# Attention features and a feed-forward block on one core: projections in 64-row tiles, query features turned on VectorE, key features on GpSimd, and one list of tasks

## The chip, the cores and the metric

The kernel runs on one core of one Trainium2 chip. The metric is the device time of one launch in microseconds (us). Three runs of the kernel before gave 123.22, 123.42 and 123.79 us; the median is 123.42 us.

## The reference, cut to what matters

```python
# q, k, v: (B=4, H=4, S=1088, D=32); S1, S2: (8, 32); all fp32
def phi(x):                                   # 64 features of a token and head
    a = einsum('rd,bhsd->bhsr', S1, x)        # 8 numbers
    b = einsum('rd,bhsd->bhsr', S2, x)        # 8 numbers
    return outer(a, b).reshape(..., 64)
q_p, k_p = phi(q), phi(k)
kv  = einsum('bhsf,bhsd->bhfd', k_p, v)       # 64 x 32 for a batch and head
z   = sum(k_p, axis=2)                        # 64
num = einsum('bhsf,bhfd->bhsd', q_p, kv)
den = einsum('bhsf,bhf->bhs', q_p, z)[..., None] + 1e-06
x   = (num / den).transpose(0, 2, 1, 3).reshape(4352, 128)
h   = x @ w_in                                # 128 x 2048
out = (h * sigmoid(h)) @ w_out                # 2048 x 128, fp32 out
```

## The kernel before

There are four batches of 1088 tokens. The keys and queries of a batch are loaded as `Kx[b]` and `Qx[b]`, 128 partitions (4 heads x 32 rows) by 34 x 32 numbers. VectorE transposes them in blocks of 32 x 32 (`transpose_cols`, L154) to `KT` and `QT`, in which the partitions hold 4 heads x 32 features. TensorE projects them with weights of 128 x 32 (`project_k` L203, `project_q` L210) in four column groups, and VectorE turns the result back to tokens on partitions (`tokens`, L218). VectorE forms the key features `kp` by a product with broadcast operands (`outer`, L194, 2304 numbers on each partition for a batch), TensorE sums `kv` over tokens (`sum_kv`, L234). The denominators come from a third set of query weights `WQb`, made from the sum of the keys (`sum_z`, `query_weights`, `mask_weights`). The query features `qp` are formed on VectorE, turned by TensorE with an identity (`turn`, L263, 72 instructions in all), copied out of PSUM by VectorE (`qpt`), multiplied with `KVbd` on TensorE (`numerators`, L274) and copied by VectorE to `xT` (128 x 4352, bf16), the input of the feed-forward block.

The feed-forward block goes over `xT` in chunks of 256, 512, 320, six times 512, and 192 tokens. A chunk has steps (`Chunk.hidden`, L317): a pair of matmuls into one of two PSUM buffers `h_ps`, a SiLU on ScalarE of 1024 numbers on each partition (fewer in the short chunks) into one of eight buffers `g`; `Chunk.output` (L329) sums the output in `o_ps`; at a chunk's end VectorE turns it (L341) and `store` issues four DMAs or more on SyncE's queue (L301).

The order is written out by hand. The code before step 0 of `feed_forward` makes the first 256 tokens; the rest of batch 0 and batches 1 to 3 are generators that are advanced once a step, beginning at steps 0, 5, 19 and 35. Every engine's instructions stand in the trace in the order in which the code issues them (`tc.manual_schedule()`).

The loads: `begin` (L82) starts a DMA that may wait for another one's landing. SyncE's queue has the keys and queries, the values of batch 0 and `w_in`; from batch 1 on each load waits for one before it. GpSimd's queue has memsets, then `w_out` (cast to bf16 by the DMA), then the values of batches 1, 2 and 3 (`load_v`, L140), where batch 1 waits for the last half of `w_in`, batch 2 for the queries of batch 1, and batch 3 for the queries of batch 2. Nothing stands behind them on GpSimd:

```python
    prev = wi1
    for b in range(1, B):
        load_v(nc.gpsimd, b, Vb[b], prev)
        kb = load_kq(nc.sync, b, k, Kx, after=prev)
        prev = load_kq(nc.sync, b, q, Qx, after=q0b if b == 1 else kb)
```

Of the kernel before, what the change touches and what calls it, by code (L numbers as in the profile page):

```python
# [9 lines left out]
FP32 = mybir.dt.float32  # L10
# [6 lines left out]
def bcast(ap: AP, axis: int, count: int) -> AP:  # L17
    pairs = [list(p) for p in ap.ap]
    pairs.insert(axis, [0, count])
    return AP(tensor=ap.tensor, offset=ap.offset, ap=pairs)  # L20
# [3 lines left out]
def kernel(  # L24
# [11 lines left out]
    nc = tc.nc  # L36
    P = nc.NUM_PARTITIONS

    B, H, S, D = q.shape
    R = S1.shape[0]  # L40
    HR = H * R
# [5 lines left out]
    NY = S // 32  # L47
    NC = 9
    YA = 24
    assert DM == P and HR == 32 and S == 32 * NY and 3 * NC < NY <= 4 * NC  # L50

    const = ctx.enter_context(tc.tile_pool(name="const", bufs=1))
    work = ctx.enter_context(tc.tile_pool(name="work", bufs=2))
    moeg = ctx.enter_context(tc.tile_pool(name="moeg", bufs=8))
    outb = ctx.enter_context(tc.tile_pool(name="outb", bufs=2))
    psH = ctx.enter_context(tc.tile_pool(name="psH", bufs=2, space=bass.MemoryType.PSUM))
    psO = ctx.enter_context(tc.tile_pool(name="psO", bufs=1, space=bass.MemoryType.PSUM))
    psP = ctx.enter_context(tc.tile_pool(name="psP", bufs=2, space=bass.MemoryType.PSUM))
    psA = ctx.enter_context(tc.tile_pool(name="psA", bufs=1, space=bass.MemoryType.PSUM))

    ctx.enter_context(tc.manual_schedule())

    Kx = [const.tile([P, NY, D], FP32, name=f"Kx{b}") for b in range(B)]
    Qx = [const.tile([P, NY, D], FP32, name=f"Qx{b}") for b in range(B)]
    Vx = const.tile([P, H, NC, D], FP32, name="Vx")
    Vb = [const.tile([P, H, NC, D], BF16, name=f"Vb{b}") for b in range(B)]
    KT = [const.tile([P, 4 * NC * 32], FP32, name=f"KT{i}") for i in range(2)]
    QT = [const.tile([P, 4 * NC * 32], FP32, name=f"QT{i}") for i in range(2)]
    PQ = [const.tile([P, 3, NC, HR], FP32, name=f"PQ{i}") for i in range(2)]
    AW = [const.tile([P, NC * H, R + 1], FP32, name=f"AW{i}") for i in range(2)]  # L70
    WQb = [const.tile([P, HR], FP32, name=f"WQb{b}") for b in range(B)]
    KVbd = [const.tile([P, 2, 2 * D], BF16, name=f"KVbd{b}") for b in range(B)]
    w_in_f = const.tile([P, DFF], FP32, name="w_in_f")
    w_in_bf = const.tile([P, DFF], BF16, name="w_in_bf")
    w_out_bf = const.tile([P, NJ, P], BF16, name="w_out_bf")
    xT = const.tile([P, NTOK], BF16, name="xT")

    S12 = const.tile([R, 2, D], FP32, name="S12")  # L80

    def begin(eng, dst, src, after=None):  # L82
        ins = eng.dma_start(dst, src)  # L83
        if after is not None:
            tc.add_manual_dep(ins.ins, after.ins.name, mybir.DependencyInfo(
                mybir.DependencyClass.Sync, mybir.DependencyReason.DATA), reason="order of loads")
        return ins

    def load_kq(eng, b, src, dst, y0=0, y1=NY, after=None):
        return begin(eng, dst[b][:, y0:y1, :].rearrange("p a d -> p (a d)"),  # L90
                     AP(tensor=src.tensor, offset=src[b, 0, y0].offset,
                        ap=[[NY * D, P], [1, (y1 - y0) * D]]), after)

    def load_v(eng, b, dst, after=None):
        for c in range(4):
            n = min(NC, NY - c * NC)
            ins = begin(eng, dst[32 * c: 32 * (c + 1), :, :n, :].rearrange("p h n d -> p h (n d)"),
                        AP(tensor=v.tensor, offset=v[b, 0, c * NC].offset,
                           ap=[[NY * D, 32], [S * D, H], [1, n * D]]), after)
        return ins  # L100

    nc.scalar.dma_start(S12[:, 0, :], S1)
    nc.sync.dma_start(S12[:, 1, :], S2)
    k0a = load_kq(nc.sync, 0, k, Kx, 0, 2 * NC)
    k0b = load_kq(nc.scalar, 0, k, Kx, 2 * NC, NY)
    q0a = load_kq(nc.sync, 0, q, Qx, 0, YA)
    v0 = load_v(nc.sync, 0, Vx, k0a)
    half = DFF // 2
    wi0 = begin(nc.sync, w_in_f[:, :half], moe_w_in[:, :half], q0a)
    wi1 = begin(nc.sync, w_in_f[:, half:], moe_w_in[:, half:])  # L110
    q0b = load_kq(nc.sync, 0, q, Qx, YA, NY, v0)


    warm = const.tile([P, 1], FP32, name="warm")
    nc.gpsimd.memset(warm, 0.0)
    ident32 = const.tile([32, 32], FP32, name="ident32")
    make_identity(nc, ident32)
    hmask = const.tile([P, H, R], FP32, name="hmask")
    nc.gpsimd.memset(hmask, 0.0)
    for h in range(H):  # L120
        nc.gpsimd.memset(hmask[D * h: D * (h + 1), h, :], 1.0)
    nc.gpsimd.memset(KT[0][:, NY * 32:], 0.0)
    nc.gpsimd.memset(QT[0][:, NY * 32:], 0.0)
    nc.gpsimd.memset(Vx[96:P, :, NY - 3 * NC: NC, :], 0.0)
    nc.gpsimd.memset(KVbd[0], 0.0)
    for i in range(2):
        nc.gpsimd.memset(AW[i][:, :, R:], 1e-6)
    ident_bf = const.tile([P, P], BF16, name="ident_bf")
    make_identity(nc, ident_bf)
    nc.gpsimd.memset(KT[1][:, NY * 32:], 0.0)  # L130
    nc.gpsimd.memset(QT[1][:, NY * 32:], 0.0)
    for b in range(1, B):
        nc.gpsimd.memset(KVbd[b], 0.0)
        nc.gpsimd.memset(Vb[b][96:P, :, NY - 3 * NC: NC, :], 0.0)
    wo = begin(nc.gpsimd, w_out_bf, moe_w_out.rearrange("(j p) m -> p j m", p=P), v0)


    prev = wi1
    for b in range(1, B):
        load_v(nc.gpsimd, b, Vb[b], prev)  # L140
        kb = load_kq(nc.sync, b, k, Kx, after=prev)
        prev = load_kq(nc.sync, b, q, Qx, after=q0b if b == 1 else kb)

    nc.scalar.activation(out=warm, in_=warm, func=ACT.Silu)
    REP32 = const.tile([32, 4, 32], FP32, name="REP32")
    nc.vector.tensor_copy(out=REP32, in_=bcast(ident32[:, :], 1, 4))
    rep32 = REP32.rearrange("p h d -> p (h d)")
    REPJ = const.tile([R, 4, R], FP32, name="REPJ")
    nc.vector.tensor_copy(out=REPJ, in_=bcast(ident32[:R, :R], 1, 4))
    hm = const.tile([HR, H], FP32, name="hm")  # L150
    nc.vector.tensor_reduce(out=hm, in_=ident32.rearrange("p (h j) -> p h j", h=H),
                            axis=AX.X, op=ALU.add)

    def transpose_cols(dst, src, b, c0, c1):  # L154
        nc.vector.transpose(out=dst[:, c0:c1],  # L155
                            in_=src[b].rearrange("p a d -> p (a d)")[:, c0:c1])


    st_ps = psA.tile([P, 2 * R], FP32, name="st_ps", tag="acc")
    nc.tensor.transpose(st_ps[:D, 0:R], S12[:, 0, :], ident32[:R, :R])  # L160
    nc.tensor.transpose(st_ps[:D, R:2 * R], S12[:, 1, :], ident32[:R, :R])
    ST_sb = const.tile([D, 2 * R], FP32, name="ST_sb")
    nc.vector.tensor_copy(out=ST_sb, in_=st_ps[:D, :])
    rep_ps = psP.tile([P, 2 * R], FP32, name="rep_ps", tag="proj")
    nc.tensor.matmul(rep_ps, rep32, ST_sb, start=True, stop=True)
    s2_ps = psA.tile([HR, D], FP32, name="s2_ps", tag="acc")
    nc.tensor.matmul(s2_ps, REPJ.rearrange("p h j -> p (h j)"), S12[:, 1, :],
                     start=True, stop=True)
    transpose_cols(KT[0], Kx, 0, 0, 2 * NC * 32)
    WK = const.tile([P, 2, H, R], FP32, name="WK")  # L170
    for i in range(2):
        nc.vector.tensor_tensor(out=WK[:, i], in0=bcast(rep_ps[:, i * R: (i + 1) * R], 1, H),  # L172
                                in1=hmask, op=ALU.mult)
    wk = [WK[:, i].rearrange("p h i -> p (h i)") for i in range(2)]
    transpose_cols(KT[0], Kx, 0, 2 * NC * 32, S)


    L1 = const.tile([HR, H, D], FP32, name="L1")
    nc.vector.tensor_tensor(out=L1, in0=bcast(s2_ps[:, :], 1, H), in1=bcast(hm[:, :], 2, D),
                            op=ALU.mult)  # L180
    l4_ps = psA.tile([P, P], FP32, name="l4_ps", tag="acc")
    L4 = const.tile([P, P], FP32, name="L4")

    def l4():
        nc.tensor.matmul(l4_ps, rep32, L1.rearrange("p h d -> p (h d)"), start=True, stop=True)  # L185
        nc.scalar.activation(out=L4, in_=l4_ps, func=ACT.Copy)  # L186

    def vcopy(out_, in_):
        nc.vector.tensor_copy(out=out_, in_=in_)  # L189

    def acopy(out_, in_):
        nc.scalar.activation(out=out_, in_=in_, func=ACT.Copy)

    def outer(dst, a, bb):  # L194
        nc.vector.tensor_tensor(  # L195
            out=dst.rearrange("p n h i j -> p (n h) i j"),
            in0=bcast(a.rearrange("p n (h i) -> p (n h) i", h=H), 3, R),
            in1=bcast(bb.rearrange("p n (h j) -> p (n h) j", h=H), 2, R), op=ALU.mult)

# [343 lines left out]
```

## Time and profile before

| what | value |
|---|---|
| median of 3 runs | 123.42 us (123.22 to 123.79) |
| profiled execution, first to last instruction (span) | 122.1 us; no time of its own is given beside it, and the median of the runs is 1.3 us longer |
| PE, DVE, ACT, POOL busy | 97.7, 68.7, 74.2, 11.8 us |
| SiLU on ACT (L325): busy, idle before them | 67.7 us in 72, 31.1 us |
| first SiLU starts, last one ends | 19.18 us, 116.91 us |
| mean granted TensorE clock | 0.983 |

PE is TensorE, DVE is VectorE, ACT is ScalarE, POOL is GpSimd, SP is SyncE. Matmuls are pipelined: a pair of 512 columns shows 0.59 us from the first start to the last end while pairs follow each other every 0.43 us, so busy time of PE is not work at its peak.

### The profile page before, as it was taken

What the parts mean: (1) busy time and instruction counts of PE and PEld (TensorE: products, weight loads), DVE (VectorE), ACT (ScalarE), POOL (GpSimd) and SP (SyncE); (2) the same over time, 40 slices, a digit from 0 to 9 for tenths busy, and PEclk for the clock granted to TensorE, in tenths of its full rate; (3) what the DMA queues carried; (4) which work ended last, traced back from release to release, by engine and by line L of the source; (5) the groups of instructions that cost most, each with busy time, mean ns of one, the idle gap of its engine ahead of it and who ended that gap; (6) DMA issues with size and microseconds to landing.
All of it is one profiled execution on the core that took longest, in us unless ns stands there. A gap on an engine that the chain in (4) does not pass through costs nothing.

```text
span 122.1 us, 2269 instructions
## 1 busy us (share of the span) xinstructions
PE 97.7 (80%) x884; PEld 50.5 (41%) x896; DVE 68.7 (56%) x126; ACT 74.2 (61%) x83; POOL 11.8 (10%) x41
## 2 busy tenths in 40 slices
PE   0397849969999649899982999999838989989940
PEld 0265627644445435435432244445304434434630
DVE  1367693499945996993369649953398430020210
ACT  4005466666576725466981379667843899999920
POOL 6604510701600000000000000000000000000000
PEclk9999999999999999999999599999999999999998
DMA  2799997691994500030013000500031005013151
GB/s 52 263 222 319 182 358 127 195 205 62 222 173 109 87 2 0 2 57 0 3 21 65 0 0 5 86 0 5 0 59 27 0 0 86 0 21 53 17 94 27
DMA packets 24314, 9.80 MB, mean 80 GB/s; under 512 B 21104, under 2 KB 22896, under 8 KB 24304
## 3 DMA queue, kind: packets, MB, share of 16 engines
q1 hardware_dynamic: 20352, 8.03, 26.0%
q0 software_dynamic: 3792, 1.36, 9.8%
q10 hardware_dynamic: 160, 0.26, 0.6%
q8 instruction: 7, 0.11, 0.4%
q14 instruction: 3, 0.02, 0.1%
HBM read 8.78 MB, written 2.23 MB: 90 GB/s over the span
## 4 chain that ended last, share of the span: by engine, by line
PE 59%; DVE 22%; ACT 7%; DMA 5%; issue 4%; SPq 0%; DVEq 0%; ACTq 0%
PE h_ps L322 20%; PE o_ps L335 17%; DVE qp L195 7%; ACT g L325 5%; PE qpt_ps L268 4%; PE pq_ps L214 3%; PE num_ps L277 3%; PE pk_ps L206 3%; DMA Kx<-in_k_dram 3%; DVE o_tt L341 3%; PE h_ps L206 2%; DVE PQ L219 2%; DVE qpt L189 2%; DVE den L256 2%; DVE AW L254 2%
## 5 line engine op out<-in xcount | busy, mean ns | idle before, releaser
L325 ACT ACTIVATE g<-h_ps 128x1024 bf16<-128x1024 f32 (+2 forms) x72 | 67.7, 980 | 31.1 <-PE h_ps L322 25.5
L322 PE MATMUL h_ps<-xT,w_in_bf 128*128 128x512 bf16 (+3 forms) x151 | 41.5, 365 | 1.9 <-ACT g L325 1.4
L335 PE MATMUL o_ps<-g,w_out_bf 128*128 128x512 bf16 (+3 forms) x157 | 39.3, 349 | 0.5
L335 PEld LDWEIGHTS <-w_out_bf 128*128 128x128 bf16 x160 | 15.5, 98 | 14.8 <-issue 1.1
L322 PEld LDWEIGHTS <-w_in_bf 128*128 128x128 bf16 x160 | 13.1, 103 | 15.9 <-issue 11.1
L341 DVE STREAM_TRANSPOSE o_tt<-o_ps 128x512 f32<-128x512 f32 (+3 forms) x10 | 6.3, 631 | 20.6 <-PE o_ps L335 18.8
L268 PE MATMUL qpt_ps<-ident_bf,qp 128*128 128x128 bf16 (+1 forms) x72 | 6.7, 235 | 9.2 <-DVE qp L195 8.5
L195 DVE TENSOR_TENSOR kp<-pk 128x1280 bf16<-128x1280 f32 (+1 forms) x8 | 10.8, 1352 | 0.2
L195 DVE TENSOR_TENSOR qp<-aqs,PQ 128x1024 bf16<-128x1024 f32 (+3 forms) x9 | 10.8, 1223 | 0.2
L268 PEld LDWEIGHTS <-qp 128*128 128x128 bf16 (+1 forms) x72 | 5.0, 106 | 12.8 <-DVE qp L195 10.0
L189 DVE COPY qpt<-qpt_ps 128x1024 bf16<-128x1024 bf16 (+2 forms) x11 | 5.9, 540 | 5.7 <-PE qpt_ps L268 5.7
L189 DVE CAST xT<-num_ps 128x512 bf16<-128x512 f32 (+2 forms) x11 | 5.8, 531 | 4.8 <-PE num_ps L277 4.8
L83 POOL DMA_DIRECT2D Vb<-in_v_dram x12 | 6.5, 548 | 15.1 <-DMA Qx<-in_q_dram 12.3
L155 DVE STREAM_TRANSPOSE KT<-Kx 128x1088 f32<-128x1088 f32 (+2 forms) x5 | 5.4, 1075 | 2.1 <-DMA Kx<-in_k_dram 2.1
L277 PE MATMUL num_ps<-qpt,KVbd 128*64 128x512 bf16 (+3 forms) x24 | 4.7, 383 | 2.2 <-DVE qpt L189 1.4
L155 DVE STREAM_TRANSPOSE QT<-Qx 128x512 f32<-128x512 f32 (+3 forms) x8 | 5.7, 718 | 0.0
L277 PEld LDWEIGHTS <-KVbd 128*64 128x64 bf16 x24 | 1.9, 111 | 7.0 <-issue 6.9
L214 PE MATMUL pq_ps<-QT,WK 128*32 128x128 f32 (+2 forms) x112 | 4.7, 284 | 0.0
L206 PE MATMUL h_ps<-KT,WK 128*32 128x160 f32 (+1 forms) x32 | 2.8, 448 | 2.1 <-DVE WK L172 2.1
L206 PE MATMUL pk_ps<-KT,WK 128*32 128x160 f32 (+1 forms) x96 | 4.2, 292 | 0.1
L186 ACT ACTIVATE L<-l_ps 128x128 f32<-128x128 f32 x1 | 0.3, 277 | 6.3 <-PE l_ps L185 6.3
L219 DVE STREAM_TRANSPOSE PQ<-pq_ps 128x256 f32<-128x256 f32 (+2 forms) x7 | 3.3, 470 | 1.0 <-PE pq_ps L214 1.0
(73 smaller groups left out, 61.6 us busy)
## 6 DMA issues: line engine op xcount, KB each, us to landing
Kx<-in_k_dram SPq DMA_DIRECT2D x3, 544.0 KB, 4.8
Qx<-in_q_dram SPq DMA_DIRECT2D x3, 544.0 KB, 6.1
out_dram<-o_tt SPq DMA_DIRECT2D x20, 64.0 KB, 1.9
w_in_f<-in_moe_w_in_dram SPq DMA_DIRECT2D x2, 512.0 KB, 6.1
Vb<-in_v_dram POOLq DMA_DIRECT2D x9, 72.0 KB, 3.8
w_out_bf<-in_moe_w_out_dram POOLq DMA_DIRECT2D x1, 512.0 KB, 8.2
Vx<-in_v_dram SPq DMA_DIRECT2D x3, 144.0 KB, 2.8
Qx<-in_q_dram SPq DMA_DIRECT2D x1, 384.0 KB, 4.9
```

Source lines behind the costliest of these rows:

```text
L83: ins = eng.dma_start(dst, src)
L155: nc.vector.transpose(out=dst[:, c0:c1], in_=src[b].rearrange("p a d -> p (a d)")[:, c0:c1])
L189: nc.vector.tensor_copy(out=out_, in_=in_)
L195: nc.vector.tensor_tensor(out=dst.rearrange("p n h i j -> p (n h) i j"), in0=bcast(a.rearrange("p n (h i) -> p (n h) i", h=H), 3, R), in1= ...
L206: nc.tensor.matmul(ps[32 * c: 32 * (c + 1), i, :], w, kt[:, (c * NC + n0) * 32: (c * NC + n1) * 32], start=True, stop=True, tile_position= ...
L214: nc.tensor.matmul(ps[32 * c: 32 * (c + 1), i, :].rearrange("p (n x) -> p n x", x=32), w, q4[:, n0:n1, c, :], start=True, stop=True, tile_ ...
L268: nc.tensor.transpose(qpt_ps[:, p, (n - n0) * P: (n - n0) * P + np_], qp[:np_, n, 2 * p: 2 * p + 2].rearrange("p h i j -> p (h i j)"), ide ...
L277: nc.tensor.matmul(num_ps[64 * p: 64 * (p + 1), :ncol], KVbd[b][:, p, :], qpt[:, p, :ncol], start=True, stop=True, tile_position=(0, 64 * p))
L322: nc.tensor.matmul(h[:, i, :self.ntok], w_in_bf[:, j * P: (j + 1) * P], xT[:, self.t0: self.t0 + self.ntok], start=True, stop=True)
L325: nc.scalar.activation(out=self.view(g)[:, :, :self.ntok], in_=h[:, :, :self.ntok], func=ACT.Silu)
L335: nc.tensor.matmul(self.o_ps[:, :self.ntok], w_out_bf[:, j, :], self.view(self.gs[s])[:, i, :self.ntok], start=(j == 0), stop=(j == NJ - 1))
L341: nc.vector.transpose(out=o_tt[:, :self.ntok], in_=self.o_ps[:, :self.ntok])
```

## The change

The kernel function is written anew. All work becomes named tasks in a table (`Order`), and one list of names gives the order in which they are issued.

- **Keys.** `KT` as before; `WK` has 128 rows and 32 columns, and the projection takes 64 rows at a time (tile position 64r, 32c: eight matmuls of 288 columns) into a pair of PSUM banks, `ap_`. Two transposes bring it to tokens (`TK`). The key features are GpSimd products (`KP`): four ninths of batch 0, and all of batches 1 to 3 in three parts of 768 numbers.
- **Queries.** One projection of 64 x 64 tiles gives both factors and the denominator's (`WQ` holds the three sets). The product `QP` is turned by a VectorE transpose of bf16 pairs as 32-bit words (`TN`), with no TensorE turn and no copy; the numerators take even and odd features apart (eight matmuls), for which the kv sums are sorted by a selection matrix `SEL`. The copies to `xT`, of the key sums and of kv are on ScalarE.
- **GpSimd's order.** Memsets, the values of batches 1 to 3 with the waits that they had, then `SEL`, four copies to `WQ`, then the products and the casts of `w_out`.
- **Loads.** `w_out` comes as fp32 on SyncE's queue ahead of batch 1 (behind `w_in`), and GpSimd casts it. Batch 1's values and keys wait for it in place of `w_in`.
- **Chunks.** 320, seven times 512, and 448 tokens. The rest of batch 0 and batches 1 to 3 are one queue of 139 tasks that is spread evenly over the steps between the chunks that need them: 11 tasks in chunk 0, 40 in chunk 1, and then 10, 29, 10, 29, 10. Outputs lag by five steps in chunk 0 and by two afterwards.
- **Warm-up.** Four matmuls of zeros at the start, five short ones before the first step.

```diff
+    wo0 = after(nc.sync.dma_start(*wo_rows(0, NJ // 4)), wi0)
+    wo1 = nc.sync.dma_start(*wo_rows(NJ // 4, NJ // 2))
...
-    prev = wi1
+    prev = wo1
     for b in range(1, B):
         load_v(nc.gpsimd, b, Vb[b], prev)
-        kb = load_kq(nc.sync, b, k, Kx, after=prev)
-        prev = load_kq(nc.sync, b, q, Qx, after=q0b if b == 1 else kb)
+        kb = load_rows(nc.sync, k, Kx, b, 0, NY, prev)
+        prev = load_rows(nc.sync, q, Qx, b, 0, NY, q0b if b == 1 else kb)
...
+    nc.gpsimd.tensor_copy(out=view(SEL[:, :], 0, (P, 2), (64, 2), (1, 64)),
+                          in_=view(ident[:, :], 0, (1, 2), (0, 2), (2, 64)))
...
+    for b in range(B):
+        nc.gpsimd.tensor_copy(out=view(WQ[b][:, :], 0, (32, 2), (8, 2), (1, 8)),
+                              in_=view(WK[:, :], 0, (8, 2), (16, 2), (1, 8)))
...
+            def project_k(y0=y0, y1=y1):
+                for c in range(y0 // NC, -(-y1 // NC)):
+                    for r in range(2):
+                        mm(ap_[32 * c: 32 * (c + 1), r * CH: r * CH + NC * 32],
+                           WK[64 * r: 64 * (r + 1), :],
+                           kt[64 * r: 64 * (r + 1), c * NC * 32: (c + 1) * NC * 32],
+                           pos=(64 * r, 32 * c))
...
+        for eng, n0, n1 in kn:
+            o.add(f"KP{b}.{n0}", lambda eng=eng, n0=n0, n1=n1: times(
+                eng, kp[:, n0 * 256: n1 * 256].rearrange("p (n i j) -> p n i j", i=8, j=8),
+                view(tk[:, :], n0 * 32, (8, 4 * (n1 - n0)), (1, 8), (0, 8)),
+                view(tk[:, :], (NC + n0) * 32, (8, 4 * (n1 - n0)), (0, 8), (1, 8))))
...
+            o.add(f"TN{b}.{p}", lambda at=at, rn=rn: nc.vector.transpose(
+                out=qu[:, at * 64: (at + rn) * 64].bitcast(FP32),
+                in_=qp[:, at * 64: (at + rn) * 64].bitcast(FP32)))
...
+    batch(0, [(0, YA), (YA, NY)], [("D", 0, 5), ("P", 5, 9)], [(0, 5), (5, 13), (13, 17)], "AAA", "A")
+    for b in range(1, B):
+        batch(b, [(0, NY)], [("P", 0, 3), ("P", 3, 6), ("P", 6, 9)], [(0, 8), (8, 17)], "AA", "A")
...
+        ks = [f"KT{b}.0", f"PK{b}.0", f"TK{b}.0", f"TK{b}.1", f"ZS{b}", f"ZT{b}"]
+        for n0 in (0, 3, 6):
+            ks += [f"KP{b}.{n0}"]
+        ks += [f"QT{b}.{p}" for p in range(pieces)]
+        ks += [f"MW{b}", f"WM{b}"] + [f"PQ{b}.0", f"TQ{b}.0"]
+        ks += [f"KV{b}.{n0}" for n0 in (0, 3, 6)] + [f"KM{b}", f"SE{b}", f"KC{b}"]
+        for p in range(pieces):
+            if p:
+                ks += [f"PQ{b}.{p}", f"TQ{b}.{p}"]
+            ks += [f"{x}{b}.{p}" for x in ("AW", "RD", "RC", "AQ", "QP", "TN", "NM", "XC")]
...
+    head = (["KT0.0", "PK0.0", f"KT0.{YA}", f"PK0.{YA}", "QT0.0", "TK0.0", "TK0.1", "ZS0", "ZT0",
+             "KP0.5", "KP0.0", "MW0", "WM0", "vb0", "PQ0.0", "TQ0.0",
+             "AW0.0", "RD0.0", "RC0.0", "AQ0.0", "wi.0", "KV0.0", "KV0.5", "KM0", "SE0", "KC0", "QP0.0", "TN0.0",
+             "NM0.0", "XC0.0", "wi.1", "fill3", "fill2"])
```

The names, each with the batch and a part: KT, QT transposes on VectorE; PK, PQ projections on TensorE; TK, TQ turns to tokens on VectorE; ZS, MW (TensorE), ZT (ScalarE), WM (VectorE) the denominator's weights; KP the key features; KV, SE (TensorE), KM (VectorE), KC (ScalarE) the kv sums; AW, RD, RC, AQ the denominators and the division, QP the query features, TN their turn (all VectorE); NM the numerators (TensorE), XC the copy to `xT` (ScalarE); H, A, O a step's hidden matmuls, SiLU and output matmuls; F a chunk's end.

## The prediction

> **What bounds the kernel now.** I read the page's slices first, then the costliest groups, then the waits, then the timeline of each queue. On the page:
>
> ```profile
> ACT  4005466666576725466981379667843899999920
> POOL 6604510701600000000000000000000000000000
> ...
> PE 59%; DVE 22%; ACT 7%; DMA 5%; issue 4%; SPq 0%; DVEq 0%; ACTq 0%
> ...
> L325 ACT ACTIVATE g<-h_ps 128x1024 bf16<-128x1024 f32 (+2 forms) x72 | 67.7, 980 | 31.1 <-PE h_ps L322 25.5
> ```
>
> ScalarE's 67.7 us of SiLU is the largest work that can't overlap itself. From the first SiLU (19.18) to the last one's end (116.91) 97.7 us pass; the rest is ScalarE waiting, 25.5 us of it for hidden matmuls. TensorE does those late because it stands in order behind attention work: the waits give "PE qpt_ps L268 <- DVE qp L195: 8.5, 5, 2.4". From 102.6 us on, with no attention left, eight steps take 7.44 us. So three stretches set the time: 19.2 us of head, 97.7 us of steps, 5.2 us of tail (116.91 to 122.1). The runs' median lies 1.3 us above the span; I add 1.3 at the end.
>
> What decides this change is an engine that is nearly idle now. The timeline of GpSimd:
>
> ```profile
> 13.65 2.16 POOL L83 DMA_DIRECT2D Vb<-in_v_dram  x4 [2.82 <-DMA w_in_f<-in_moe_w_in_dram]
> 21.61 2.14 POOL L83 DMA_DIRECT2D Vb<-in_v_dram  x4 [5.80 <-DMA Qx<-in_q_dram]
> 30.21 2.17 POOL L83 DMA_DIRECT2D Vb<-in_v_dram  x4 [6.46 <-DMA Qx<-in_q_dram]
> ```
>
> The columns are start, time, engine and line; the bracket is the idle time and what ended it. GpSimd itself stands still until the queries of batches 1 and 2 have landed, and is free only at 32.4 us. Now nothing is queued behind. That a queue holds what is behind a waiting load is seen on SyncE's, whose first store of output follows the last loads, though VectorE had that output ready at 27.4 us (26.97 + 0.44):
>
> ```profile
> 29.67 0.33 SPq L83 DMA_DIRECT2D Kx<-in_k_dram  x1
> 33.45 0.33 SPq L83 DMA_DIRECT2D Qx<-in_q_dram  x1
> 33.83 18.99 SPq L301 DMA_DIRECT2D out_dram<-o_tt  x12
> ```
>
> **The change, term 1: when GpSimd gets to its new work.** In the changed code the three groups of value loads stay where they were, with their waits, and behind them come `SEL`, the `WQ` copies and the key features of batch 0, `KP0.5`. `PQ0.0` needs `WQ`; the first tokens need it, `SEL` and `KP0.5`. So the head waits for the queries of batch 2. The load chain itself also moves: batch 1's values and keys now wait for `w_out`, 1024 KB as fp32, which goes by SyncE's queue behind `w_in`. Keys and values of batch 0, `w_in` and most of the queries, 2656 KB, were there by 13.4 us, some 218 KB/us from 1.2 us on; 1024 KB more are 4.7 us at that rate, 3.3 us at the 319 GB/s of the page's fourth slice. Against that `w_out` no longer runs beside batch 1's loads (7.5 us from Q1's issue to its landing, against 4.6 for Q2 alone). Bounds for the shift: 0 to 4.7 us; I take 2.1, the middle. Later loads keep their times (K2 3.7, Q2 4.6, the POOL wait 0.5, issue 2.17). GpSimd free at 32.4 + 2.1 = **34.5 us**. S2 and the second part of K0 change queues in the first 2 us, and that is nothing under this wait; the cover gone, they too are one issue each of 0.36 us.
>
> **Term 2: from there to the first SiLU.** `SEL` and the `WQ` copies: 256 and 4x32 numbers; POOL memsets give 0.31 for 256 and 0.11 for little: 0.95 with handovers. `KP0.5`, 1024 numbers: no POOL product is in the trace. VectorE's row for that shape is 1.22 us, and POOL's dearest rate is the affine select, 292 ns for 128, or 2.3 ns a number, 2.35 us. Bounds 1.2 and 2.35; I take 2.35, being the POOL row that computes something. Then kv matmuls 0.5, mask 0.25, `QP0.0` 0.83 (768 numbers took 0.96), turn 0.5 (a 320 transpose took 0.50), numerators 0.6, copy to `xT` 0.45 (0.38 for 256), then the cast `wi.1`, 1.06, which stands ahead of the first SiLU on ScalarE. 0.95 + 2.35 + 0.5 + 0.25 + 0.83 + 0.5 + 0.6 + 0.45 + 1.06 = **7.5 us**. The query side (0.7 projection, 0.52 turn, 1.05 for four small operations) hides beside `KP0.5`. First SiLU at 42.0, against 19.18.
>
> In this wait TensorE is idle for over 20 us. The trace shows what 2.38 us of idle did at 66.4 us; the columns are the stretch, its length, the busy time of PE, weight load, DVE, ACT and POOL, the granted clock, and DMA:
>
> ```profile
> 65.00:66.00 1.00, 0.00 (x0) 0.00 (x0) 0.97 (x2) 0.00 (x0) 0.00 (x0) 1.00 0.53 89
> 66.00:67.00 1.00, 0.62 (x9) 0.63 (x10) 1.00 (x2) 0.00 (x0) 0.00 (x0) 0.85 0.00 0
> 67.00:68.00 1.00, 1.00 (x5) 0.39 (x3) 1.00 (x2) 0.00 (x0) 0.00 (x0) 0.50 0.00 0
> 68.00:69.00 1.00, 1.00 (x5) 0.13 (x2) 0.32 (x1) 0.90 (x1) 0.00 (x0) 0.50 0.00 0
> ```
>
> A pair of hidden matmuls took 0.96 to 1.06 there, against 0.59. In my head the matmuls are already costed at the slow head's durations, so I add nothing; 1 us is in the range. The Trainium skill, "TensorE: Matmul & The Clock Gate", Part 1, has the clock halved after about 3.4 us of idle and full again only after as long a busy stretch. By it the warm-up at the start is lost whole, and later stalls under 3.4 us cost nothing; the rows show a shorter stall that did cost, about 1.5 us in all. By the page the sum stays as it is; by the rows one such stall in each of batches 1 to 3 would make it 4.5 us longer, which is within the range.
>
> **Term 3: the steps.** SiLU work: 8 of 640 at 0.70, 56 of 1024 at 1.03 (0.93 at the end), 8 of 896 at 0.92 (between 0.82 for 768 and 1.03): about 70 us. The turns by TensorE (72, 6.7 us busy) and the waits for them go, and VectorE's copies (5.9 and 5.8 us), for about 1.1 us a batch of new transposes. ScalarE takes over 8 copies to `xT` of some 0.6, three of kv at 0.4 and three of key sums at 0.2: 6.8 us, on the engine with most work.
> But the tasks stand in single-buffered chains. Batch 2 in chunk 3, in order: PK 0.65, two turns 0.95, three KP of 768 numbers at 1.75 (0.9 to 1.75 by the rows above), kv sums 0.3, mask 0.25, four small operations 1.2, QP 1.23, TN 0.7, NM 0.5, XC 0.65, the next hidden pair 0.6, and twelve handovers of 0.1. VectorE's mask stands ahead of the denominators, so they wait for GpSimd. Sum 13.4 us, where eight SiLU are 8.2. Chunk 1 has batch 0's last piece ahead of such a chain (0.5 + 0.43 + 1.05 + 0.69 + 0.42 + 0.45 + 0.4 + 0.8 of handovers = 4.7) and KT (1.3), which can't run ahead: 13.4 + 4.7 + 1.3 = 19.4. Chunks 2, 4 and 6 have 10 tasks in 8 steps: 8.2 + a copy 0.65 + a hidden pair 0.6 + one stall 0.55 = 10.0. Chunk 0: QT runs ahead; hidden pair and PQ 1.1, turn 0.69, small ones 1.2, QP 1.23, TN 0.69, NM 0.5, a SiLU 0.7, XC 0.6, hidden 0.6 = 7.3. Chunks 7 and 8: 7.6 + 7.4. Sum: 7.3 + 19.4 + 3 x 10.0 + 2 x 13.4 + 7.6 + 7.4 = **98.5 us**, so the steps are no shorter than the 97.7 of before: where stalls for the TensorE turns go, GpSimd's products are late next. `w_out`'s casts on GpSimd lie before the first output (five steps of lag) and the stores before 34 us no longer wait: nothing, for the steps begin after the loads' end.
>
> **Term 4: tail** as before, 5.2. Sum: 34.5 + 7.5 + 98.5 + 5.2 = 145.7 us of span, and 1.3 around it: **147.0 us**.
>
> **Rivals.** *GpSimd isn't held*: its value loads are handed over and the copies behind run at once. Then K0 (4.98 us), its turns, the chain ZS to WM and the sum of term 2 give a first SiLU at about 15.7, 26.3 us sooner, and 147.0 - 26.3 = 120.7: faster than 123.42. It decides as soon as GpSimd is free before about 11 us. Against it: three rows put GpSimd's own idle time down to a load's landing. 8 in 100.
> *The steps run better*: GpSimd's products at 0.9 us take 0.85 x 9 = 7.7 out of term 3, and a stall a chunk less about 3 more: 136. 13 in 100.
> *The products cost double*, 3.5 us each: 9 x 1.75 = 15.8 on the chains, less some slack: 160. By the Trainium skill, "GPSIMD Engine Reference", section 1, GpSimd shares its memory interfaces with VectorE operations of two inputs. No run here shows it. The only cover is that VectorE then does mostly transposes, of one input. 8 in 100.
> The forecast as worked: 71 in 100.
>
> **Numbers.** Term 1 moves by -2.1 to +2.6, term 2 by -1.2 to +2, term 3 by -8 to +8; 137 to 157 holds my case, and reaching half into the two rivals beside it gives **136 to 159**, which leaves out the first rival. A measurement here tells 0.5% (0.6 us) from no change. Faster needs the first rival and its steps as long as worked, or shorter: 0.08; same 0.02; slower 0.90.
>
> **What would show it.** Right: a third group of value loads on POOL at about 32 us with `SEL`, `WQ` copies and a product right behind; PE, DVE and ACT empty from some 11 to 34 us in the slices; first SiLU near 42; POOL products of 768 numbers near 1.75 us, TensorE's kv matmuls waiting for them. Wrong: POOL products at 8 to 12 us, and a first SiLU before 20 us.

## The result and the profile after

The changed kernel takes 145.28 us (median of 4 runs, 144.72 to 145.37). The kernel before took 123.58 us beside it (123.22 to 123.79). The ratio is 1.171, with a 95% interval of 1.1638 to 1.1782: slower. The profiled execution took 145.37 us, with a span of 143.6 us and a mean granted clock of 0.984. Medians here are over all runs of a kernel and ratios over its undisturbed ones, so a ratio can differ a little from the quotient of two medians; the profiled executions of e1, e2 and e7 lie near the top of their runs, and only their heads, tails and single instructions are read.

First the page of the kernel after: five rows of the slices (3.6 us each), the chain by engine, and three groups.

```profile
PE   5450000005398638958887797896897895998920
DVE  1470000005847375382952573880756570101010
ACT  4024000000277551684896757797659698899920
POOL 6200325069300002900000910000740000000000
PEclk9999999999999995999999999999999999999998
...
PE 43%; DMA 18%; DVE 15%; ACT 12%; issue 4%; POOL 2%; SPq 2%; DVEq 0%; ACTq 0%; POOLq 0%
...
L407 ACT ACTIVATE G<-hp 128x1024 bf16<-128x1024 f32 (+2 forms) x72 | 67.0, 979 | 24.2 <-PE hp L106 20.4
...
L231 POOL TENSOR_TENSOR KP<-TK 128x768 bf16<-128x768 f32 (+1 forms) x10 | 15.3, 1558 | 55.4 <-DVE TK L264 55.4
...
L106 PE MATMUL pair<-QT,WQ 64*64 64x256 f32 (+3 forms) x72 | 6.5, 438 | 23.4 <-POOL WQ L217 22.3
```

TensorE and VectorE stand empty from the fourth slice to the ninth, ScalarE from the fifth to the tenth, while GpSimd works only in short pieces. DMA's share of the chain went from 5% to 18%. The SiLU work itself (67.0 us against 67.7) and ScalarE's waits for hidden matmuls (20.4 against 25.5) did not grow. The last row has the whole loss in it: 22.3 us for a copy to `WQ`, a tile of 32 numbers a row.

GpSimd's timeline shows why that copy was late:

```profile
16.65 2.34 POOL L125 DMA_DIRECT2D Vb<-in_v_dram  x4 [12.24 <-DMA w_out_f<-in_moe_w_out_dram]
22.02 2.14 POOL L125 DMA_DIRECT2D Vb<-in_v_dram  x4 [3.03 <-DMA Qx<-in_q_dram]
30.05 2.14 POOL L125 DMA_DIRECT2D Vb<-in_v_dram  x4 [5.88 <-DMA Qx<-in_q_dram]
32.23 0.40 POOL L202 CAST SEL<-ident 128x256 bf16<-128x256 f32 x1
32.58 0.67 POOL L217 COPY WQ<-WK 128x32 f32<-128x32 f32 x4
33.20 1.96 POOL L231 TENSOR_TENSOR KP<-TK 128x1024 bf16<-128x1024 f32 x1
35.10 2.05 POOL L228 CAST w_out_bf<-w_out_f 128x1024 bf16<-128x1024 f32 x2
```

`SEL`, the copies and the first product depend on nothing that is late, and they run right behind the third group of value loads. ScalarE's timeline gives the first SiLU and the last five:

```profile
40.23 0.70 ACT L407 ACTIVATE G<-hp 128x640 bf16<-128x640 f32 x1
...
132.98 4.15 ACT L407 ACTIVATE G<-hp 128x896 bf16<-128x896 f32 x5 [0.41 <-PE hp L106]
```

So the head is 40.2 us (19.2 before), the steps 137.13 - 40.23 = 96.9 us (97.7), the tail 143.6 - 137.13 = 6.5 us (5.2). The change of the span, 21.5 us, is +21.0 - 0.8 + 1.3. The steps hardly gained, although the turns by TensorE and the waits for them are gone. The waits name what came in their place:

```profile
PE pair L106 <- POOL WQ L217: 22.3, 1, 22.3
...
PE pair L106 <- DVE QU L352: 6.7, 6, 1.8
PE hp L106 <- ACT xT L224: 5.3, 7, 1.3
...
PE small L106 <- POOL KP L231: 0.9, 1, 0.9
```

The columns are microseconds in all, times, and the longest. TensorE now waits for VectorE's turned features (`QU`, 6.7 us; before, for `qp`, 8.5) and for ScalarE's copies to `xT`. For GpSimd's products it waits once, in the head.

### The profile page after: what moved, and what is told of

It is laid out like the page before. It is cut to its first block, busy times and chain, and to the rows that moved or that the text cites. A ratio compares the mean times of both kernels' runs of the same rounds, so it can differ in the third digit from the quotient of the medians.

```text
span 143.6 us, 1853 instructions
## 1 busy us (share of the span) xinstructions
PE 89.4 (62%) x667; PEld 38.7 (27%) x677; DVE 57.3 (40%) x108; ACT 77.2 (54%) x94; POOL 28.1 (20%) x56
## 4 chain that ended last, share of the span: by engine, by line
PE 43%; DMA 18%; DVE 15%; ACT 12%; issue 4%; POOL 2%; SPq 2%; DVEq 0%; ACTq 0%; POOLq 0%
PE op L106 16%; PE hp L106 15%; PE pair L106 8%; ACT G L407 8%; DMA Qx<-in_q_dram 6%; DMA Kx<-in_k_dram 4%; DVE OT L423 4%; DMA w_out_f<-in_moe_w_out_dram 4%; DMA w_in_f<-in_moe_w_in_dram 4%; PE small L106 3%; DVE QP L231 3%; ACT xT L224 3%; DVE QU L352 2%; POOL Vb L125 1%; DVE AW L231 1%
## 5 line engine op out<-in xcount | busy, mean ns | idle before, releaser
L407 ACT ACTIVATE G<-hp 128x1024 bf16<-128x1024 f32 (+2 forms) x72 | 67.0, 979 | 24.2 <-PE hp L106 20.4
L106 PE MATMUL hp<-xT,w_in_bf 128*128 128x512 bf16 (+2 forms) x140 | 41.2, 377 | 6.1 <-ACT xT L224 5.3
L106 PE MATMUL op<-G,w_out_bf 128*128 128x512 bf16 (+2 forms) x138 | 39.8, 371 | 3.5 <-DVE OT L423 2.6
L231 POOL TENSOR_TENSOR KP<-TK 128x768 bf16<-128x768 f32 (+1 forms) x10 | 15.3, 1558 | 55.4 <-DVE TK L264 55.4
L332 DVE STREAM_TRANSPOSE TQ<-pair 128x512 f32<-128x512 f32 (+3 forms) x9 | 6.2, 687 | 38.4 <-PE pair L106 38.4
L106 PE MATMUL pair<-QT,WQ 64*64 64x256 f32 (+3 forms) x72 | 6.5, 438 | 23.4 <-POOL WQ L217 22.3
L423 DVE STREAM_TRANSPOSE OT<-op 128x512 f32<-128x512 f32 (+2 forms) x9 | 6.2, 688 | 21.8 <-PE op L106 21.8
L231 DVE TENSOR_TENSOR QP<-AQ,TQ 128x1024 bf16<-128x1024 f32 (+3 forms) x9 | 11.1, 1235 | 0.3
L106 PEld LDWEIGHTS pair<-QT,WQ 64*64 64x64 f32 x72 | 2.1, 147 | 25.9 <-POOL WQ L217 22.4
L224 ACT ACTIVATE xT<-pair 128x512 bf16<-128x512 f32 (+3 forms) x9 | 5.1, 570 | 2.6 <-PE pair L106 2.6
L352 DVE STREAM_TRANSPOSE QU<-QP 128x512 f32<-128x512 f32 (+3 forms) x9 | 6.1, 682 | 0.3
```

Of the source, the lines that this page charges most:

```text
L106: nc.tensor.matmul(dst, w, x, start=start, stop=stop, tile_position=pos, **kw)
L231: (nc.vector if eng == "D" else nc.gpsimd).tensor_tensor(out=out_, in0=a, in1=c, op=ALU.mult)
L332: nc.vector.transpose(out=tq[:, at * 32: (at + 2 * m) * 32], in_=view(ap_[:, :], 0, (CH, 2), (1, m * 32)))
L352: o.add(f"TN{b}.{p}", lambda at=at, rn=rn: nc.vector.transpose(out=qu[:, at * 64: (at + rn) * 64].bitcast(FP32), in_=qp[:, at * 64: (at + ...
L407: nc.scalar.activation(out=view(gb[:, :], 0, (stride, per), (1, ntok)), in_=view(hb[:, :], 0, (stride, per), (1, ntok)), func=ACT.Silu)
L423: nc.vector.transpose(out=OT[kk % 2][:, :ntok], in_=op[:, :ntok])
```

## The experiments

Two questions were open: whether it is the order of GpSimd's queue that holds the head (and not the loads themselves, or GpSimd's speed), and why the steps are no shorter once the head is mended.

### The head

**e1: the value loads become tasks behind GpSimd's work.** The waits on `w_out` and on the queries stay; only the place in the queue changes.

```diff
-        load_v(nc.gpsimd, b, Vb[b], prev)
+        vdep[b] = prev
...
+    for v_, x_ in (("V1", "KP0.5"), ("V2", "wo.1"), ("V3", "KP1.6")):
+        names.insert(names.index(x_) + 1, v_)
```

> The changed kernel with the value loads of batches 1, 2 and 3 moved behind GpSimd's head work (the first behind KP0.5, the second behind the second cast of w_out, the third behind KP1.6); nothing else differs. Theory (GpSimd stood behind waiting loads): SEL, WQ and KP0.5 run at 8 to 12 us, first SiLU near 16 us against 40.2, the steps as long as before (97 us from first to last SiLU), the time about 145.3 - 24 = 121, faster than the kernel before by some 2%. Rival (the head is long because the loads land late: w_out as fp32 ahead of batch 1): first SiLU stays above 35 us and the time above 140.

125.48 us (123.85 to 126.72), ratio 1.0099 (1.0051 to 1.0147). The first SiLU starts at 16.93 us, 23.3 us sooner than after the change, on the same loads. The head's theory stands. But the total fell by only 20 us. GpSimd's timeline, and then VectorE's, show a cost that the place in the queue brought with it:

```profile
9.36 3.26 POOL L234 TENSOR_TENSOR KP<-TK 128x1024 bf16<-128x1024 f32 x1 [2.99 <-DVE TK L267]
18.24 2.34 POOL L125 DMA_DIRECT2D Vb<-in_v_dram  x4 [5.63 <-DMA w_out_f<-in_moe_w_out_dram]
20.57 2.03 POOL L231 CAST w_out_bf<-w_out_f 128x1024 bf16<-128x1024 f32 x2
```

```profile
9.31 1.49 DVE L234 TENSOR_TENSOR KP<-TK 128x1280 bf16<-128x1280 f32 x1
...
19.73 3.02 DVE L234 TENSOR_TENSOR AQ<-TQ,DN 128x128 f32<-128x128 f32 x1
22.79 1.22 DVE L234 TENSOR_TENSOR QP<-AQ,TQ 128x1024 bf16<-128x1024 f32 x1
```

`AQ`, a product of 128 numbers, took 3.02 us and ended 0.15 us after GpSimd's two casts (22.75 against 22.60). It began 0.84 us ahead of their shown start, while GpSimd issued value loads; since `AW`, at 18.78 us under the same issues, took only 0.29, these rows don't tell what held `AQ` before 20.57. And the key product on GpSimd, 1.96 us in the kernel after, took 3.26 beside VectorE's product of 1.49 us.

**e2: only the third group is moved.** The same edit with `V3` alone, behind `KP1.6`. If the order holds the head, the gain is the time between the second and the third group.

> The changed kernel with only the third group of value loads moved (behind KP1.6); the first two stay ahead of GpSimd's head work with their waits. Theory: GpSimd is free when the second group is issued, 22.0 + 2.1 = 24.2 us by the changed kernel's trace, in place of 32.2; everything after it moves by 8.0 us: first SiLU near 32.2, time near 137.3. Rival (late loads): no change from 145.3.

138.4 us (137.06 to 139.5), ratio 1.115 (1.1052 to 1.1248). GpSimd's timeline:

```profile
23.10 2.14 POOL L125 DMA_DIRECT2D Vb<-in_v_dram  x4 [3.14 <-DMA Qx<-in_q_dram]
25.29 0.40 POOL L205 CAST SEL<-ident 128x256 bf16<-128x256 f32 x1
```

`SEL` starts 6.9 us sooner (25.29 against 32.23), the first SiLU 7.0 (33.28 against 40.23), and the median falls by 6.9. One group moved, its share of the wait gone; all moved, all gone. The time between the second and the third group was 8.0 us; the gain is 1.1 less because the loads came that much later in this run (the second group at 23.10 against 22.02).

**e3: batch 1's values and keys wait for `w_in` again.** It isolates the shift that the prediction put on `w_out`.

```diff
-    prev = wo1
+    prev = wi1
```

> The changed kernel, in which the loads of batch 1 wait for the last half of w_in (as before the change) and not for w_out; the order of SyncE's queue stays. If w_out's way costs the 2.1 us of the prediction's first term, batch 2's queries land 2 us sooner and the time is near 143.3. If, as the trace of the changed kernel suggests (GpSimd free at 32.2 against 32.4 before), that detour costs nothing because the same bytes must come anyway, the time stays within 0.5 us of 145.3.

143.68 us (143.07 to 147.8), ratio 1.1597 (1.1501 to 1.1692).

```profile
12.06 2.34 POOL L125 DMA_DIRECT2D Vb<-in_v_dram  x4 [7.66 <-DMA w_in_f<-in_moe_w_in_dram]
20.79 2.15 POOL L125 DMA_DIRECT2D Vb<-in_v_dram  x4 [6.39 <-DMA Qx<-in_q_dram]
28.44 2.14 POOL L125 DMA_DIRECT2D Vb<-in_v_dram  x4 [5.50 <-DMA Qx<-in_q_dram]
```

GpSimd is free at 30.6 us in place of 32.2: the wait for `w_out` costs 1.6 us. Batch 1's group goes out 4.6 us sooner, and the next comes 8.7 us behind it in place of 5.4, because `w_out` is now carried beside batch 1's keys and queries.

**e4: batch 0's last key product on VectorE.** `("P", 5, 9)` becomes `("D", 5, 9)`: is GpSimd's slower product what the head pays?

> The changed kernel with batch 0's second part of the key features (KP0.5) on VectorE, where it can run at about 10 us in the long wait. Takes KP0.5 (1.96 us on GpSimd) out of the head's chain, which then goes by the query side. If VectorE's two-input operations were slowed by GpSimd working beside them (AW0.0 took 0.99 us during KP0.5, QP0.0 1.45 during the cast of w_out, where the same kinds cost about 0.25 and 0.83), AW0.0 drops to about 0.25 and the first SiLU comes 1.0 to 1.8 us sooner: 143.5 to 144.3. If AW0.0's length has another cause it stays near 1 us and the gain is under 0.7.

146.62 us (144.37 to 148.56), ratio 1.1732 (1.16 to 1.1864): not told apart from the changed kernel's 1.171. The first SiLU came 0.57 us sooner (39.66). The casts of `w_out` moved up to 33.32 us, and VectorE's `AW`, 0.27 us in e1, took 1.03 beside them; `QP`, with GpSimd idle by then, took 0.82 in place of 1.45. So the speed of GpSimd's product is under a microsecond of the head; the queue is the rest.

**e5: e1, and the casts of `w_out` on VectorE.** It tests what held `AQ` in e1.

```diff
-        o.add(f"wo.{i}", lambda i=i: copy("P", w_out_bf[:, i * half: (i + 1) * half],
+        o.add(f"wo.{i}", lambda i=i: copy("D", w_out_bf[:, i * half: (i + 1) * half],
```

> The kernel with the value loads behind GpSimd's head work, and the two casts of w_out on VectorE in place of GpSimd; nothing else differs. With the casts on GpSimd AQ0.1, a VectorE product with two operands in SBUF, took 3.02 us (0.29 elsewhere) and ended 0.15 us after the second cast; the SiLU behind it waited 2.78 us, and TensorE, idle for 2.4 us, then ran at half clock for some 4 us. Theory (VectorE's two-operand products stand still while GpSimd works): AQ0.1 back to 0.3, that gap under 1 us, 2.7 + about 2 us off, about 1.4 us of casts added on VectorE beside other waits: 120 to 121.5, against 124 to 125.5 with the casts on GpSimd. Rival (AQ0.1 waited for something else, and the chain is bound elsewhere): no faster than 123.5.

123.4 us (122.26 to 125.39), ratio 0.9986 (0.9937 to 1.0035), about 2 us short of what the theory promised. (The stretch at half clock that the theory names lasts 6.8 us in e1, from 25.82 us on, rather than 4.) VectorE's timeline:

```profile
20.06 0.63 DVE L229 CAST w_out_bf<-w_out_f 128x1024 bf16<-128x1024 f32 x1
20.61 0.28 DVE L234 TENSOR_TENSOR AQ<-TQ,DN 128x128 f32<-128x128 f32 x1
```

`AQ` is back at 0.28 us without the casts on GpSimd, and a cast costs VectorE 0.65 where it cost GpSimd 1.02. GpSimd is idle by then, for its value loads are issued by 19.43, so this run doesn't tell the casts from the issues. The span, 122.1 us, is the one of the kernel before, differently made up: head 16.9 (19.2), steps 98.8 (97.7), tail 6.3 (5.2). With the head mended the change is worth nothing, and that is the second question.

### The steps

A chunk's length is the time from its first SiLU to the next chunk's first. In e5 they are 9.1, 18.1, 11.5, 12.5, 10.2, 12.5, 10.2 us, and 14.8 for the last two: the chunks with 29 or 40 tasks (1, 3 and 5) are over the 8.2 us of their SiLU by 4.3 to 10 us.

**e6: even pace.** e5, with the tasks spread over pairs of chunks rather than due in one: if the chunks with 29 tasks are long because their tasks are squeezed, spreading them should shorten the pairs.

```diff
-            want = start + -(-(target - start) * (s + 1) // ns)
+            marks = [(0, 0), (16, 51), (32, 90), (48, 129), (56, 139), (99, 139)]
+            for (a0, w0), (a1, w1) in zip(marks, marks[1:]):
+                if a0 < nstep + 1 <= a1:
+                    want = w0 + -(-(w1 - w0) * (nstep + 1 - a0) // (a1 - a0))
```

> As e5, and the 139 tasks are spread evenly: 51 over the 16 steps of chunks 0 and 1 (11 and 40 before), 39 over each following pair of chunks (10 and 29 before). Theory (the steps of chunks 1, 3 and 5 are long because the chain of a batch is issued just in time, 18.3, 12.5 and 12.5 us where 8 SiLU are 8.2, while chunks 0, 2 and 4 wait little): chunks 2 to 5 come to about 10.5 us each in place of 10.2 and 12.5, chunks 0 and 1 to about 23 together in place of 26.5, in all 5 to 7 us less than e5: 114 to 116. Rival (the length of the chains, not their place, sets the time: TensorE stands in every link in order): within 2 us of e5.

126.56 us (126.24 to 126.96), ratio 1.0282 (1.0229 to 1.0335): longer. Chunks 0 and 1 took 29.3 us (27.1 in e5), 2 and 3 24.6 (24.0), 4 and 5 23.2 (22.7). Chunks 0 and 1 don't compare the pace alone: TensorE's matmuls, slow at the start of every kernel here, become fast at 34.65 us in e6 and at 19.40 in e5 (the last section says how that is read). Chunks 4 and 5 have full clock in both, and there a task's wait costs as much in a step of an easy chunk. The squeeze was not it.

**e7: a short end.** e6, with the last 448 tokens as 256 and 192.

> As e6, with the last 448 tokens as two chunks of 256 and 192. After the last SiLU the changed kernel needed 6.5 us (448 tokens left to sum, turn and store), the kernel before 5.2 (192 tokens). If the tail goes by the last chunk's size, 1.0 to 1.3 us less than e6, less some 0.3 for one more chunk's end; if the tail is the store's landing and the end of the program, no change.

123.58 us (122.44 to 126.05), ratio 0.9958 (0.9905 to 1.0011). From the last SiLU's end to the span's end: 4.8 us, where e6 has 6.1. So the longer tail comes from the 448-token end, 1.3 us. What makes up the rest of the 3 us between the medians of e6 and e7 stays open; the edit wasn't shown to cause it.

**e8: the key features of batches 1 to 3 on VectorE.** e6 with `"P"` changed to `"D"` in three places. Are GpSimd's products on the steps' path?

> As e6, with the key features of batches 1 to 3 on VectorE in place of GpSimd (three products of 768 numbers each; by the rows of this case about 0.95 us each on VectorE, 1.48 on GpSimd). If GpSimd's products are late on the chain (the prediction's third term), the batches' chains get shorter by up to 1.6 us each and the time falls by 2 to 4 us. If they are hidden (TensorE waited 0.9 us for one of them in the changed kernel, in the head, and for none in the steps), the move adds 2.9 us of work a batch to VectorE's queue ahead of the query side: 0 to 4 us slower than e6.

125.26 us (124.81 to 125.56), ratio 1.0182 (1.0125 to 1.0238). A product of 768 numbers takes 0.95 us on VectorE and 1.51 on GpSimd, and chunks 4 and 5 are 23.1 us against e6's 23.2. In chunk 5 of both kernels the last product ends before the first sums that read it begin (84.21 and 85.34 us in e6, 79.85 and 82.88 in e8): whichever engine makes them, they are not what is late there. The median is 1.3 us under e6's; in e8's trace the slow matmuls of the start end at 28.42 us, and chunk 2, which has a stretch at half clock in e6 from 51.72 us on, has none.

**e9: the hidden matmuls one step ahead.** e5, with H of the next step issued right behind A of this one and ahead of the tasks, so that a SiLU doesn't wait for a hidden matmul that stands behind a waiting task.

```diff
-            names.append(f"H{kk}.{s}")
+            if s == 0:
+                names.append(f"H{kk}.0")
             names.append(f"A{kk}.{s}")
+            if s + 1 < ns:
+                names.append(f"H{kk}.{s + 1}")
```

> As e5 (the tasks paced as in the changed kernel), but a step's hidden matmuls stand on TensorE ahead of the tasks of the step before it, so that ScalarE has the next input while TensorE waits for a link of a chain; at a chunk's first step they can't, since its input comes from the tasks. Theory (spreading the tasks gained nothing because every link makes TensorE wait in order with the next hidden matmuls behind it, whatever the step): the waits of 0.3 to 1.2 us before the SiLU within a chunk go, 2 to 3 us in each of chunks 3 and 5, about 1 in 2, 4 and 6, 3 to 5 in 0 and 1: 98.8 us from first to last SiLU come to 87 to 90, the time to 112 to 115. Rival (the chains' own length sets chunks 1, 3 and 5): those chunks stay above 12 us and the time above 119.

121.63 us (120.97 to 122.49), ratio 0.9841 (0.9783 to 0.9899): faster, but far less than the theory promised, and inside what the rival said (chunks 3 and 5 above 12 us, the time above 119). ScalarE's waits for hidden matmuls fell from 26.3 us (e5) to 11.7, and the time didn't follow. Chunk lengths are 8.4, 18.8, 9.4, 12.9, 9.4, 12.9, 9.4 and about 15: the easy chunks gained 0.8, chunks 3 and 5 lost 0.4. ScalarE's timeline through chunks 4 and 5, and the start of 6:

```profile
66.58 3.99 ACT L410 ACTIVATE G<-hp 128x1024 bf16<-128x1024 f32 x4 [0.74 <-PE hp L106]
70.89 3.77 ACT L410 ACTIVATE G<-hp 128x1024 bf16<-128x1024 f32 x4 [0.32 <-PE hp L106]
74.53 0.68 ACT L227 ACTIVATE xT<-pair 128x576 bf16<-128x576 f32 x1
75.95 1.94 ACT L410 ACTIVATE G<-hp 128x1024 bf16<-128x1024 f32 x2 [0.74 <-PE hp L106]
78.45 0.20 ACT L227 ACTIVATE ZT<-small 128x32 f32<-128x32 f32 x1 [0.57 <-PE small L106]
78.55 1.95 ACT L410 ACTIVATE G<-hp 128x1024 bf16<-128x1024 f32 x2
80.88 1.02 ACT L410 ACTIVATE G<-hp 128x1024 bf16<-128x1024 f32 x1 [0.37 <-PE hp L106]
83.08 1.02 ACT L410 ACTIVATE G<-hp 128x1024 bf16<-128x1024 f32 x1 [1.18 <-PE hp L106]
...
87.52 0.60 ACT L227 ACTIVATE xT<-pair 128x512 bf16<-128x512 f32 x1 [0.78 <-PE pair L106]
88.85 3.98 ACT L410 ACTIVATE G<-hp 128x1024 bf16<-128x1024 f32 x4 [0.74 <-PE hp L106]
```

Chunk 4's eight SiLU run in two unbroken groups (66.58 to 74.66); chunk 5's have gaps still (75.95 to 86.7), and a copy to `xT` and a hidden pair stand between the chunks. The waits show VectorE idle 9.0 us in three waits for tokens of a query projection that stands behind the next chunk's first hidden matmuls: the hidden matmuls no longer wait for the tasks, and a task waits for them. That is a part of it only: of the last of these waits (86.99 to 89.97) four hidden matmuls take 1.0 us, and the numerators, the copy to `xT` and the projection itself the rest.

**e10: e9 with e7's short end.**

> As e9 with the last 448 tokens as chunks of 256 and 192. After the last SiLU e7 took 4.8 us where e6 took 6.1; the same 1.3 us here, less 0.3 for one more chunk: about 1 us faster than e9.

120.65 us (120.15 to 121.59), ratio 0.9767 (0.9711 to 0.9822): about 1 us under e9, as expected. The tail is 5.3 us against e9's 6.4, and the last chunks take 0.35 us more. It beats both kernels.

**e11: e10 with the key features of batches 1 to 3 on VectorE.**

> As e10 with the key features of batches 1 to 3 on VectorE. Here the chains are closer to the bound. If GpSimd's products (1.48 us each, 4.45 a batch) are the late link, VectorE's (0.95 each) bring 1 to 3 us; if VectorE's queue is what the chain goes by (it then has 2.9 us more a batch ahead of the query side), 1 to 3 us slower; as between e6 and e8, whose undisturbed chunks were equally long, within 1 us.

126.26 us (125.57 to 126.7), ratio 1.0218 (1.0175 to 1.0261): 5.6 us above e10. With the hidden matmuls ahead, GpSimd's share counts. By shape, and from the waits:

```profile
L234 DVE TENSOR_TENSOR KP<-TK 128x768 bf16<-128x768 f32 x9 | 8.2, 946 | 0.1
```

```profile
PE pair L106 <- DVE WQ L234: 4.9, 4, 2.5
```

VectorE has 8.2 us of products more, and what stands behind them on VectorE comes later: TensorE waits 4.9 us for `WQ` (1.5 in e10). Chunks 3 and 5 take 14.3 and 14.2 us (12.9 in e10). Chunk 1 takes 20.9 (18.3), but a stretch at half clock lies in it (from 36.76 us on), which e10 has in chunk 2.

**e12: e10 with e6's even pace.**

> As e10 with the even pace of e6 (51 tasks over chunks 0 and 1, 39 over each following pair of chunks). In e10 chunks 3 and 5 stayed at 12.9 us with the hidden matmuls ahead, chunks 2, 4 and 6 fell to 9.4: a chain of 29 tasks in 8 steps is too long for them. If the chain's length in too few steps is what is left, 12 steps for it take 2 us from each pair of chunks (22.3 now) and the time comes to 115 to 118. If each link costs its wait wherever it stands, as between e5 and e6, the pairs stay above 21.8 us and the time within 2 us of 120.65.

121.96 us (119.86 to 123.43), ratio 0.9754 (0.97 to 0.9808), not told apart from e10. A pair of chunks takes 22.4 us in place of 9.4 + 12.9 = 22.3. With the tasks spread, the easy chunk takes what the hard one gives. Chunks 4 and 5 together take 22.7 us in e5, 23.2 in e6, 22.3 in e9 and 22.5 in e12, so neither the pace nor the hidden matmuls' place moves the sum by more than 0.9 us.

**What stays open.** Two chunks have 16 SiLU of 1.02 us, about 16.4 us (15.1 where they follow each other without a gap, four in 3.77 us), and on ScalarE about 1.9 us of copies (0.60 + 0.68 to `xT`, 0.38 + 0.2 of sums). What fills the pair to 22.3 us is, by the trace, links in series: `PK`, `TK`, `PQ`, `TQ`, `NM` and `XC` all go through the one tile `ap_`, and each engine takes its tasks in one order. That reading is argued from the code and the waits. A kernel with a second `ap_` wasn't tried, so it isn't shown.

## Why the prediction was right, and where not

The forecast was 147.0 us, and 145.37 was measured in the profiled execution. The main case happened: GpSimd's new work stands behind three waiting groups of loads. By terms, with the difference from the forecast:

| term | forecast | measured | difference |
|---|---|---|---|
| GpSimd free | 34.5 | 32.2 | -2.3 |
| from there to the first SiLU | 7.5 | 8.0 | +0.5 |
| steps | 98.5 | 96.9 | -1.6 |
| tail | 5.2 | 6.5 | +1.3 |
| around the span | 1.3 | 1.8 | +0.5 |
| sum | 147.0 | 145.4 | -1.6 |

The sum came closer than its parts, since two misses stand against three.

**Term 1, mis-sized.** The shift was bounded by 0 and 4.7 us, and 2.1 was taken as the middle, which is 2.35; it was -0.2. The three groups of loads show it in steps: the first goes out 3.0 us later than before (16.65 against 13.65), the second follows it 2.6 us sooner (5.37 against 7.96), the third 0.6 sooner (8.03 against 8.60). The prediction named the relief, `w_out` no longer beside batch 1's loads, with its rows (7.5 us against 4.6), and then left it out of the sum: a shift below zero was never in the bounds. e3 gives the wait alone, 1.6 us.

**Term 2, two errors that nearly cancel.** The first key product took 1.96 us, not 2.35. But the small operations that were to hide beside it could not, and the casts of `w_out`, costed at nothing because the first output comes five steps later, held `QP`. VectorE's timeline in the kernel after:

```profile
34.27 0.99 DVE L231 TENSOR_TENSOR AW<-TQ 128x80 f32<-128x80 f32 x1
...
36.37 1.45 DVE L231 TENSOR_TENSOR QP<-AQ,TQ 128x640 bf16<-128x640 f32 x1
```

They take 0.27 and 0.81 us in e1's head, where GpSimd is at its product's end or idle. `AW` ends 0.10 us after GpSimd's product (35.26 against 35.16) and `QP` 0.67 after its casts (37.82 against 37.15). The due time of the casts was the wrong thing to look at; what they run beside was the right one.

**Term 3, right in its result and wrong in one reason.** The chunk lengths were 8.2, 18.3, 10.2, 12.5, 10.2, 12.5, 10.2 and 14.8; forecast were 7.3, 19.4, 10.0, 13.4, 10.0, 13.4, 10.0 and 15.0. By its own rows batch 2's chain adds up to 13.5, not 13.4, and the copies on ScalarE to 6.6, not 6.8, which moves the sum by less than 0.3. So the single-buffered chains were costed about right, and "the steps are no shorter" holds. But "GpSimd's products are late next" fell: TensorE waited for them once, for 0.9 us, in the head, and e8 shows that in its chunks 4 and 5 it makes no difference which engine has them. In the kernel after they are close, though: in chunk 3 the last product ends at 83.16 us and the sums that read it begin at 83.40. Three products of 768 took 4.45 us, not 5.25, which is as large as most of the 0.9 that chunks 3 and 5 came in under; that it is the cause isn't shown. Late next were the turned features and the copies to `xT`, in their order on TensorE.

**Term 4, mis-sized.** "Tail as before" overlooked that the last chunk is now 448 tokens; e7 puts 1.3 us on that, e10 1.1.

**The clock.** Nothing was added for it, and 1 us kept in the range. TensorE was idle for 22 us; the query projection of 256 columns at 40.06 us then took 1.13 us, and 0.66 from 59 us on. In e5, whose TensorE works in every slice of its head, the same one took 1.13 too. So the slow head was only moved, as costed. One dip came in chunk 1, read here by stretches of 1 us (the columns as in the prediction):

```profile
52.00:53.00 1.00, 0.70 (x4) 0.16 (x2) 0.70 (x2) 0.21 (x1) 0.00 (x0) 1.00 0.00 0
53.00:54.00 1.00, 0.00 (x0) 0.00 (x0) 1.00 (x1) 1.00 (x2) 0.00 (x0) 0.77 0.22 39
54.00:55.00 1.00, 0.84 (x16) 0.24 (x16) 0.01 (x1) 0.09 (x1) 0.00 (x0) 0.50 0.48 82
55.00:56.00 1.00, 1.00 (x10) 0.28 (x3) 0.46 (x2) 0.00 (x0) 0.00 (x0) 0.50 0.26 44
56.00:57.00 1.00, 0.77 (x2) 0.15 (x1) 1.00 (x4) 0.00 (x0) 0.53 (x1) 0.52 0.00 0
```

TensorE was idle for 1.46 us there, and at half clock for 3.4 us or so; a key projection took 1.21 us against 0.71 at 76.78 us. The Trainium skill, "TensorE: Matmul & The Clock Gate", Part 1, has the clock halved after an idle window of about 3.4 us. This row differs: the clock fell at about 53.5 us, 0.85 us into the idle time, and in the 3.4 us before that TensorE had been busy for 1.3, with one earlier gap of 1.25 us; no window of 3.4 us stood idle. The measurement decides, and a stall of 1.5 us in a chunk may cost another microsecond behind it.

**The rivals.** *GpSimd isn't held* (120.7): refuted by the timeline after, and e1 has the state that it described, with a first SiLU at 16.9 us, not 15.7, and 125.48 us, for the held products and the longer tail weren't in it. *The steps run better* (136): it needed products of 0.9 us and fewer stalls; the products ran at 1.51 us rather than 1.75, TensorE didn't wait for them in the steps, and the steps took 96.9 us. *Products cost double* (160): they took 1.51 us each, so no; yet the mechanism it named is real (below): it cost `QP` 0.6 us in the head after the change, and `AQ` 2.7 us in e1.

## What to carry to other kernels

Before giving work to an engine that looks idle, read its own queue: a load that waits there is work in front, and its wait (22.3 us here) goes to whatever is queued behind, however small. When a wait is removed from an in-order chain, expect the next link to show it, and measure sums over whole stretches: chunks 4 and 5 kept their 22 to 23 us through four kernels while, from e5 to e9, ScalarE's waits for hidden matmuls fell by more than half. When a transfer is moved, count what it no longer runs beside as well as who now waits for it, and let the bounds go below zero.

## What the runs showed of the hardware that was not expected

**GpSimd and VectorE's products take turns.** A VectorE product of two SBUF operands that started while GpSimd worked ended 0.10 to 0.15 us after GpSimd's instruction in the plainest cases: `AW` 0.99 us for 0.27 under a product, `AW` in e4 1.03 for 0.27 under a cast, and `AQ` 3.02 for 0.28 in e1, which ended with two casts of 1.02. The other way round, GpSimd's product took 3.26 us for 1.96 beside a VectorE product of 1.49. `KM`, a VectorE product whose first operand lies in PSUM, was not held: 0.28 us under a cast (at 36.17 us after the change) and 0.29 with GpSimd idle (at 84.12). These look like a stop rather than a slower rate; why `AQ` stood before its casts began stays open. The Trainium skill, "GPSIMD Engine Reference", section 1, states that GpSimd shares its SBUF interfaces with VectorE, with contention for VectorE's instructions of two SBUF inputs. The runs agree, and show how long it lasts, also where GpSimd's instruction is a cast with one input.

**A granted clock of 1.00 where none was recorded.** After the change a pair of hidden matmuls of 320 columns took 0.69 us at 39.44 us and 0.43 at 44.12, and the view shows 1.00 for both. The trace's first record of the clock stands at 43.31 us, and the view counts all time before it as 1.00. In every kernel of this case the hidden matmuls become faster at that first record, at 22.33 us before the change, 19.40 in e5 and 34.65 in e6. So the means of the granted clock count the slow matmuls of the start as full speed; the duration of a known form shows them.
